# Padded layout for six chunks instead of four, more zero matmuls in the opening, and two weight casts split over two engines

## Chip, cores, metric

The kernel runs on one core of one Trainium2 chip. The metric is device time in microseconds (us) of one execution. Each comparison ran before and changed kernel in turn on one chip. A profile is one execution under the hardware profiler; its "span" is a little shorter than the device time (219.3 against 221.05 us for the profiled run of before).

## The reference, cut to what matters

Block-wise attention with a decay per head is followed by a feed-forward layer with SiLU. There are 4 batches, 8 heads, 768 positions, head size 64; the reference walks blocks of 64 positions.

```python
for b in range(nb):
    intra = einsum('bhic,bhjc->bhij', qb, kb) * Dmask      # scores in the block
    intra = einsum('bhij,bhjd->bhid', intra, vb)
    inter = einsum('bhid,bhde->bhie', qb * lam_pow, kv_state)
    out[:, :, sl] = intra + inter
    kv_state = lam_block * kv_state + einsum('bhsd,bhse->bhde', kb * rev_pow, vb)
...
h = x @ w_in                                               # x is [3072, 512]
out = (h * sigmoid(h)) @ w_out                             # w_in [512, 2048], w_out [2048, 512]
```

## The kernel before

The kernel works on 24 chunks of 128 tokens, six to a batch. The decay sits in the queries and keys beforehand, so a chunk's attention is: transposes of queries and keys ("tq", "tk", "tp"), scores ("sp", then masked into "ss"), state ("kv_ps", moved to "kvbd"), outputs ("op", moved to "xt"). Two heads share the 128 partitions, so keys and values need zeros beside them. There are two layouts:

- Padded: for each head of a pair a full 128-key tile in which the other head is zero ("ktbd"); the values ("vpad") have zero halves. Both score matmuls are 128 columns wide, and one cast puts the values in place.
- Halves: the tiles hold half the keys of both heads. The second matmul of each kind is 64 columns wide, which saves TensorE (in the trace of before these follow each other every 0.029 us, those of 128 columns every 0.056). But the values must be spread by four further VectorE copies a chunk.

The first four chunks use the padded layout (`c < N0`), the others the halves. POOL (GpSimd) clears the buffers in between.

```python
def spread_v(c):                     # halves only: four VectorE copies, 64 x 256 bf16
    if c in vnew:
        vnew.discard(c)
        vb, vh = natb[c][2], vhalf[c % NKV]
        for j in range(2):
            for h in range(2):
                nc.vector.tensor_copy(vh[64*j:64*j+64, :, h, j, :], vb[64*h:64*h+64, :, j, :])

def pe_s(c, j, tag="att"):           # scores
    qt, kt = tr[c]
    a = 0 if c < N0 else 64 * j
    ...
    for p in range(NP):
        lhsT = kt[:, p, j, :] if c < N0 else kt[:, p, j, :, :]
        nc.tensor.matmul(sp[:, p, :], lhsT=lhsT, rhs=qt[:, p, a:], start=True, stop=True)

def clear_halves():                  # POOL, after the first four chunks are issued
    for i in range(NKV):             # four buffers, used in turn: c % NKV
        nc.gpsimd.memset(ktbd[i], 0.0)
        nc.gpsimd.memset(vpad[i], 0.0)
    ...
```

The program order of the opening is written in a string. `z:8` is eight zero matmuls of 512 columns which only keep TensorE busy, `pq`/`pk` prepare queries and keys, `m` masks, `w:0,D` casts the first piece of `w_in` on VectorE (D), `f:part,half` is an opening feed-forward group: `part` picks two of the four chunks, `half` the two weight slices ("pieces" 0 and 1) it needs.

```
z:8 pq:0,1,P pq:0,0,D tq:0,h pk:0,D pk:1,P tk:0,o z:1 kt:0,1,D ...
... m:3,1,D w:0,D d:2 kv:2,A o:2,att x:2,D
d:3 o:3,att f:0,0 x:3,A w:1,D kv:3,A f:0,1 f:1,0 f:1,1 w:2,D w:3,D
```

After the opening come the feed-forward of chunks 0 to 3, then chunks 4 and 5 between its down-projections, then chunks 6 and 7 between the matmuls of the next feed-forward group, and so on:

```python
st_s(5)
vcast(4), vcast(5)
spread_v(4), spread_v(5)
down0(3, 2)
...
st_o(5)
next_prep()                          # POOL: queries and keys of a later chunk
down0(3, 1)
...
stretch((ups(1), 0, 1), ([(vcast, 6), (spread_v, 6)], 0.0, 0.1), (pieces(2), 0.2, 1.15), ...)
```

## Time and profile before

| | |
|---|---|
| device time, median of the first 3 runs (and of 6) | 221.94 us (222.09) |
| profiled span | 219.3 us |
| TensorE busy | 205.9 us |
| TensorE busy in 50-60 us | 6.91 of 10 us |

The head of the profile's page gives each engine's busy time and share of the span:

```profile
span 219.3 us, 4154 instructions
...
PE 205.9 (94%) x1595; PEld 127.4 (58%) x1595; DVE 122.5 (56%) x264; ACT 102.7 (47%) x213; POOL 62.1 (28%) x68
```

PE is TensorE, DVE VectorE, ACT ScalarE. Only some 13 us of TensorE's time are open to this kind of change. The table of stretches says where a good part of them is:

```profile
core 0: us, PE busy (x) PEld busy (x) DVE busy (x) ACT busy (x) POOL busy (x), PEclk, DMA share, GB/s
50.00:60.00 10.00, 6.91 (x74) 4.80 (x71) 8.84 (x20) 4.65 (x10) 4.87 (x5) 1.00 1.29 227
60.00:70.00 10.00, 10.00 (x105) 7.65 (x102) 8.72 (x21) 5.29 (x13) 4.19 (x4) 1.00 1.26 222
```

From 60 us on TensorE is full. The timeline of TensorE (start, duration, instruction; in brackets the idle time before it and what ended it) names the gaps:

```profile
22.07 13.57 PE L417 MATMUL h_ps<-xt,w_in_bf 128*128 128x256 bf16 x72 [0.39 <-DVE w_in_bf L159]
...
50.84 0.55 PE L394 MATMUL op<-ss,vpad 128*128 128x128 bf16 x8 [0.61 <-DVE vpad L274]
...
53.54 0.40 PE L394 MATMUL op<-qt,kvbd 128*128 128x128 bf16 x4 [1.29 <-DVE kvbd L159]
...
59.56 0.51 PE L363 MATMUL sp<-qt,ktbd 128*128 128x128 bf16 x8 [1.16 <-DVE ktbd L159]
```

All four are released by VectorE. The chain of waits shows what VectorE was doing: the copies of chunk 4's and 5's values, one by one (start, duration, step):

```profile
48.77 0.79 DVE vpad L274
...
49.58 0.22 DVE vpad L274
...
49.83 0.95 DVE vpad L274
...
50.81 0.23 DVE vpad L274
```

One copy takes 0.22 us, but two took 0.79 and 0.95. The mixed timeline at chunk 6 shows with what they coincide:

```profile
55.61 1.04 POOL L243 TENSOR_TENSOR qb<-qf,lam_fwd 128x512 bf16<-128x512 f32 x1 [1.35 <-DMA qf<-in_q_dram]
55.90 2.39 DVE L274 COPY vpad<-vb 64x256 bf16<-64x256 bf16 x4
...
56.93 1.04 POOL L237 TENSOR_TENSOR kb<-kf,lam_bwd 128x512 bf16<-128x512 f32 x1 [0.27 <-DMA kf<-in_k_dram]
...
58.32 0.42 DVE L325 COPY qt<-tp 128x512 bf16<-128x512 bf16 x1
```

By the single records of this trace, 57 of the 80 value copies met no POOL instruction and took 0.22 us each. Sixteen began while one ran: fifteen of them ended 0.08 us after it and took 0.84 to 1.09 us, and one took 0.22. Seven had one start beside them and took 0.22. Here four copies of 0.22 us took 2.39 us, and the copy behind them, of chunk 6's transposed queries, waited too.

The second weight piece: the list of transfers, limited to the moment of its issue (14.9 us), gives its time from issue to landing as the last column:

```profile
w_tmp<-in_moe_w_in_dram SPq DMA_DIRECT2D x1, 512.0 KB, 5.3
```

It landed at 20.2 us.

### The profile page before, as it was taken

To read this page: it belongs to the slowest core of one execution; us is meant where nothing else is said; L and a number is where in the kernel's file an instruction comes from. 1 tells how busy PE (TensorE), PEld (TensorE's weight loads), DVE (VectorE), ACT (ScalarE), POOL (GpSimd) and SP (SyncE) were. 2 spreads that over 40 slices of the span, in tenths; PEclk is the share of its full clock that TensorE was granted. 3 is DMA by queue.
4 is the path that set the end of the run, shared out by engine and by line. 5 is a ranking of instruction groups with operands and counts; after the bars stand their busy time and mean duration, and the time that the engine had idled before them with its cause. 6 is when DMAs were issued, how large, how long until landed. Compare 5 with 4: busy or idle time off the path is not lost.

```text
span 219.3 us, 4154 instructions
## 1 busy us (share of the span) xinstructions
PE 205.9 (94%) x1595; PEld 127.4 (58%) x1595; DVE 122.5 (56%) x264; ACT 102.7 (47%) x213; POOL 62.1 (28%) x68
## 2 busy tenths in 40 slices
PE   4878999996799999999999999999999999999993
PEld 1456644553695777775665566556655565566641
DVE  7699555089888768886686564436571341100021
ACT  4685564142673555655554454445445434433300
POOL 7579600716333332323333334203000000000000
PEclk9999999999999999999999999999999999999999
DMA  4999999999999999999999999949510011011112
GB/s 122 242 221 351 381 387 341 263 232 219 234 232 187 215 194 175 220 202 197 190 173 215 240 169 233 201 115 190 107 48 34 14 51 49 0 51 48 48 56 88
DMA packets 97652, 38.03 MB, mean 173 GB/s; under 512 B 86880, under 2 KB 90976, under 8 KB 97632
## 3 DMA queue, kind: packets, MB, share of 16 engines
q1 hardware_dynamic: 97488, 37.76, 81.1%
q8 instruction: 12, 0.20, 0.4%
q14 instruction: 8, 0.07, 0.1%
q10 hardware_dynamic: 144, 0.00, 0.0%
HBM read 27.27 MB, written 6.29 MB: 153 GB/s over the span
## 4 chain that ended last, share of the span: by engine, by line
PE 83%; DVE 10%; ACT 3%; DMA 2%; issue 1%; POOL 1%; DVEq 0%
PE o_ps L443 37%; PE h_ps L417 35%; PE op L394 5%; PE sp L363 4%; DVE ss L370 3%; DVE vpad L274 2%; DMA lam_sb<-in_lam_dram 2%; PE kv_ps L339 2%; ACT g L421 1%; DVE ktbd L159 1%; DVE ob L447 1%; DVE w_in_bf L159 1%; POOL qb L232 1%; DVE vpad L159 1%; ACT L127 1%
## 5 line engine op out<-in xcount | busy, mean ns | idle before, releaser
L421 ACT ACTIVATE g<-h_ps 128x256 bf16<-128x256 f32 (+2 forms) x144 | 65.1, 456 | 79.5 <-PE h_ps L417 78.1
L417 PE MATMUL h_ps<-xt,w_in_bf 128*128 128x256 bf16 (+2 forms) x592 | 99.9, 304 | 1.0 <-DVE w_in_bf L159 0.7
L443 PE MATMUL o_ps<-w_out_bf,g 128*128 128x512 bf16 x384 | 95.8, 379 | 0.2 <-DVE w_out_bf L159 0.2
L417 PEld LDWEIGHTS <-w_in_bf 128*128 128x128 bf16 x592 | 55.4, 98 | 32.6 <-issue 1.3
L443 PEld LDWEIGHTS <-g 128*128 128x128 bf16 x384 | 36.4, 98 | 32.2 <-issue 0.3
L447 DVE COPY ob<-o_ps 128x512 f32<-128x512 f32 x24 | 16.5, 691 | 47.1 <-PE o_ps L443 47.0
L243 POOL TENSOR_TENSOR qb<-qf,lam_fwd 128x512 bf16<-128x512 f32 x18 | 19.0, 1055 | 67.9 <-DMA qf<-in_q_dram 63.3
L370 DVE TENSOR_TENSOR ss<-sp,mask 128x512 bf16<-128x512 f32 (+1 forms) x48 | 25.7, 575 | 17.2 <-PE sp L363 16.5
L274 DVE COPY vpad<-vb 64x256 bf16<-64x256 bf16 x80 | 29.0, 362 | 1.8
L237 POOL TENSOR_TENSOR kb<-kf,lam_bwd 128x512 bf16<-128x512 f32 x23 | 24.3, 1060 | 6.0 <-DMA kf<-in_k_dram 4.1
L159 DVE CAST kvbd<-kv_ps 64x256 bf16<-64x256 f32 x32 | 13.5, 421 | 9.6 <-PE kv_ps L339 9.4
L402 ACT ACTIVATE xt<-op 128x512 bf16<-128x512 f32 x20 | 11.9, 597 | 11.0 <-PE op L394 10.3
L363 PEld LDWEIGHTS <-ktbd 128*128 128x128 bf16 x192 | 11.8, 100 | 6.2 <-DVE ktbd L159 2.9
L363 PE MATMUL sp<-qt,ktbd 128*128 128x128 bf16 (+1 forms) x192 | 13.7, 213 | 1.7 <-DVE ktbd L159 1.6
L394 PE MATMUL op<-ss,vpad 128*128 128x128 bf16 (+1 forms) x192 | 12.5, 208 | 0.6 <-DVE vpad L274 0.6
L157 ACT ACTIVATE vb<-vf 128x512 bf16<-128x512 f32 x20 | 12.5, 624 | 0.7 <-DMA vf<-in_v_dram 0.6
L159 DVE COPY ktbd<-kn 64x512 bf16<-64x512 bf16 x32 | 12.2, 382 | 0.8 <-DMA kn<-kb 0.5
L394 PEld LDWEIGHTS <-vpad 128*128 128x128 bf16 x192 | 10.7, 98 | 1.1 <-DVE vpad L274 0.8
L232 POOL TENSOR_TENSOR qb<-qf,lam_fwd 128x512 bf16<-128x512 f32 x4 | 4.6, 1166 | 16.6 <-DMA qf<-in_q_dram 15.0
L394 PE MATMUL op<-qt,kvbd 128*128 128x128 bf16 x80 | 7.7, 219 | 1.3 <-DVE kvbd L159 1.3
L159 DVE CAST w_in_bf<-w_tmp 128x1024 bf16<-128x1024 f32 x8 | 6.2, 781 | 3.8 <-DMA w_tmp<-in_moe_w_in_dram 3.8
L489 PE MATMUL warm_ps<-kvbd 128*128 128x512 bf16 x11 | 5.3, 632 | 3.2 <-DVE kvbd L108 3.2
(58 smaller groups left out, 85.4 us busy)
## 6 DMA issues: line engine op xcount, KB each, us to landing
kf<-in_k_dram SPq DMA_DIRECT2D x24, 256.0 KB, 4.8
vf<-in_v_dram SPq DMA_DIRECT2D x24, 256.0 KB, 5.1
out_dram<-ob SPq DMA_DIRECT2D x24, 256.0 KB, 3.1
qf<-in_q_dram SPq DMA_DIRECT2D x18, 256.0 KB, 3.7
w_tmp<-in_moe_w_in_dram SPq DMA_DIRECT2D x8, 512.0 KB, 8.6
w_tmp<-in_moe_w_out_dram SPq DMA_DIRECT2D x8, 512.0 KB, 10.1
qf<-in_q_dram SPq DMA_DIRECT2D x3, 512.0 KB, 5.9
qt<-qb SPq DMA_TRANSPOSE x16, 3.7
```

What stands on the lines that cost most here:

```text
L157: nc.scalar.activation(dst, src, AF.Copy)
L159: nc.vector.tensor_copy(dst, src)
L237: VG[e].tensor_tensor(kb, rawk.pop(c).rearrange("s (p j) d -> s p j d", j=2), decay(lam_bwd, c % NB), op=AL.mult)
L243: nc.gpsimd.tensor_tensor(qb, rawq.pop(c).rearrange("s (p j) d -> s p j d", j=2), decay(lam_fwd, c % NB), op=AL.mult)
L274: nc.vector.tensor_copy(vh[64 * j:64 * j + 64, :, h, j, :], vb[64 * h:64 * h + 64, :, j, :])
L363: nc.tensor.matmul(sp[:, p, :], lhsT=lhsT, rhs=qt[:, p, a:], start=True, stop=True)
L370: VG[e].tensor_tensor(ss, sp, m[:, None, :n].to_broadcast([128, 4, n]), op=AL.mult)
L394: nc.tensor.matmul(dst, lhsT=lhsT, rhs=rhs, start=(i == 0), stop=(i >= len(terms) - NP), skip_group_check=True)
L417: nc.tensor.matmul(hp[:, a:z], lhsT=w_in_bf[:, ko, m * 128:(m + 1) * 128], rhs=xt[g][:, ko, a:z], start=(ko == 0 and a == 0), stop=(ko == ...
L421: nc.scalar.activation(gg, hp[:, :n], AF.Silu)
L443: nc.tensor.matmul(o, lhsT=gt[g, ko][:, mt * BLK:(mt + 1) * BLK], rhs=w_out_bf[:, ko, :], start=(ko == 0), stop=(ko == KO_OUT - 1))
L447: nc.vector.tensor_copy(ob, o)
```

## The change

Its intent: take the value copies of chunks 4 and 5 off VectorE; let TensorE reach its full clock, which in before it has from 11.9 us on, sooner and keep it; shorten VectorE's work before the first feed-forward groups. The core of the diff (every other `c < N0` becomes `c < NPAD` likewise):

```diff
+NPAD = 6
-z:8 pq:0,1,P ... pk:1,P tk:0,o z:1 kt:0,1,D ...
+z:15 pq:0,1,P ... pk:1,P z:2 tk:0,o z:2 kt:0,1,D ...        # 26 zero matmuls in all, not 11
-... m:3,1,D w:0,D d:2 kv:2,A o:2,att x:2,D
-d:3 o:3,att f:0,0 x:3,A w:1,D kv:3,A f:0,1 f:1,0 f:1,1 ...
+... m:3,1,D d:2 kv:2,A
+o:2,att x:2,D w:0,DA z:1,o d:3 o:3,att f:0,0 x:3,A w:1,DA kv:3,A f:0,1 f:1,0 f:1,1 ...
+    nc.vector.memset(kvbd[NKV - 1], 0.0)      # the zero tile, now VectorE's first instruction
     nc.gpsimd.memset(ktbd[2], 0.0)
...
     def cast_w(which, i, e="D"):
-        move(e, w_piece(...), wtmp.pop((which, i)))
+        n = dst.shape[1] // len(e)
+        for h, x in enumerate(e):             # "DA": half on VectorE, half on ScalarE
+            move(x, dst[:, n*h:n*h+n, :], t[:, n*h:n*h+n, :])
...
-        a = 0 if c < N0 else 64 * j
+        a = 0 if c < NPAD else 64 * j
...
-    clear_halves()
+    clear_halves(2, 3)
...
     vcast(4), vcast(5)
-    spread_v(4), spread_v(5)
...
     st_o(5)
     next_prep()
+    clear_halves(0, 1)
     down0(3, 1)
...
-    stretch((ups(1), 0, 1), ([(vcast, 6), (spread_v, 6)], 0.0, 0.1), (pieces(2), ...
+    stretch((ups(1), 0, 1), ([(vcast, 6)], 0.0, 0.1), ([(spread_v, 6)], 0.42, 0.42), (pieces(2), ...
```

Buffers 0 and 1 are now in use until chunk 5, so their clearing moves from the opening to a place after chunk 5.

More of the change, by code (lines that the diff above doesn't have):

```diff
@@ L21 @@
 NQ2 = 6
+NPAD = 6
 ORDER = """
-z:8 pq:0,1,P pq:0,0,D tq:0,h pk:0,D pk:1,P tk:0,o z:1 kt:0,1,D qt:0,A kt:0,0,D qt:1,A s:0,1,o tk:1,h m:0,1,D pq:2,0,D
-s:0,0,att z:2 pq:2,1,P kt:1,0,A s:1,0,o tq:2,att kt:1,1,A pk:2,P m:0,0,D qt:2,A s:1,1,h vc:0,A tk:2,att m:1,0,D
-m:1,1,D d:0 qt:3,A pk:3,P kt:2,1,D s:2,1,h kt:2,0,D kv:0,A o:0,att s:2,0,h m:2,1,D tk:3,o m:2,0,D vc:1,A d:1 x:0,A
-kt:3,0,D kv:1,A s:3,0,att o:1,att kt:3,1,D s:3,1,h vc:2,D m:3,0,D vc:3,D x:1,A m:3,1,D w:0,D d:2 kv:2,A o:2,att x:2,D
-d:3 o:3,att f:0,0 x:3,A w:1,D kv:3,A f:0,1 f:1,0 f:1,1 w:2,D w:3,D
+z:15 pq:0,1,P pq:0,0,D tq:0,h pk:0,D pk:1,P z:2 tk:0,o z:2 kt:0,1,D qt:0,A kt:0,0,D qt:1,A s:0,1,o z:1 tk:1,h m:0,1,D
+pq:2,0,D s:0,0,att z:2 pq:2,1,P kt:1,0,A s:1,0,o tq:2,att kt:1,1,A pk:2,P m:0,0,D qt:2,A s:1,1,h vc:0,A tk:2,att
+m:1,0,D m:1,1,D d:0 qt:3,A pk:3,P kt:2,1,D s:2,1,h kt:2,0,D kv:0,A o:0,att s:2,0,h m:2,1,D z:1,o tk:3,o m:2,0,D vc:1,A
+z:2,o d:1 x:0,A kt:3,0,D kv:1,A s:3,0,att o:1,att kt:3,1,D s:3,1,h vc:2,D m:3,0,D vc:3,D x:1,A m:3,1,D d:2 kv:2,A
+o:2,att x:2,D w:0,DA z:1,o d:3 o:3,att f:0,0 x:3,A w:1,DA kv:3,A f:0,1 f:1,0 f:1,1 w:2,D w:3,D
 """
@@ L106 @@
         nc.vector.memset(vpad[i], 0.0)
-        if i == 1:
-            nc.vector.memset(kvbd[NKV - 1], 0.0)
         nc.vector.memset(ktbd[i], 0.0)
@@ L161, in cast_w @@
     def cast_w(which, i, e="D"):
-        move(e, w_piece(which, i, None, w_in_bf if which == "in" else w_out_bf), wtmp.pop((which, i)))
+        dst, t = w_piece(which, i, None, w_in_bf if which == "in" else w_out_bf), wtmp.pop((which, i))
+        n = dst.shape[1] // len(e)
+        for h, x in enumerate(e):
+            move(x, dst[:, n * h:n * h + n, :], t[:, n * h:n * h + n, :])
     mask2 = const.tile([128, BLK], F32)
@@ L170, with clear_halves @@
     khalf = [t.rearrange("d p j s -> d p (j s)").rearrange("d p (h j s) -> d p h j s", h=2, j=2) for t in ktbd]
-    def clear_halves():
-        for i in range(NKV):
+    def clear_halves(*bufs):
+        for i in bufs:
             nc.gpsimd.memset(ktbd[i], 0.0)
             nc.gpsimd.memset(vpad[i], 0.0)
-        for j in range(2):
-            nc.gpsimd.tensor_copy(mask2[64 * j:64 * j + 64, :], mask[0:64, :])
     NBUF = {"att": 3, "h": 2, "o": 2, "kv": 1}
@@ L190 @@
     xt = {}
-    N0 = GROUPS[0] // BLK
     def load_q(c):
@@ L238, in prep_k @@
                                 op=AL.mult)
-        natb[c] = (None, kb, vpad[c % NKV] if c < N0 else nat.tile([128, NP, 2, D], BF16, name="vb", tag="vb", bufs=2))
+        natb[c] = (None, kb, vpad[c % NKV] if c < NPAD else nat.tile([128, NP, 2, D], BF16, name="vb", tag="vb", bufs=2))
     def prep(c):
@@ L248, in vcast @@
     def vcast(c, e="A"):
-        if c in vraw and c >= N0:
+        if c in vraw and c >= NPAD:
             vb = natb[c][2]
@@ L284, in move_k @@
         rows = slice(64 * j, 64 * j + 64)
-        if c < N0:
+        if c < NPAD:
             move(e, ktbd[c % NKV][rows, :, j, :], t[rows, :, :])
@@ L304, in copy_qt @@
              tp[:, :, :, 64 * i:64 * i + 64].rearrange("d r p s -> d p s r"))
-        tr[c] = (qt, ktbd[c % NKV] if c < N0 else khalf[c % NKV])
+        tr[c] = (qt, ktbd[c % NKV] if c < NPAD else khalf[c % NKV])
     def pe_tk(c, tag):
@@ L338, in pe_d @@
         for p in range(NP):
-            nc.tensor.matmul(kv[:, p, :], lhsT=kb[:, p, :, :], rhs=vb[:, p, 0:4:3, :] if c < N0 else vb[:, p, :, :],
+            nc.tensor.matmul(kv[:, p, :], lhsT=kb[:, p, :, :], rhs=vb[:, p, 0:4:3, :] if c < NPAD else vb[:, p, :, :],
                              start=(blk == 0 and p == 0), stop=True, skip_group_check=True)
@@ L358, in pe_s @@
         qt, kt = tr[c]
-        a = 0 if c < N0 else 64 * j
+        a = 0 if c < NPAD else 64 * j
         sp = psum.tile([128, NP, BLK - a], F32, name="sp", tag=tag, bufs=NBUF[tag], padded_shape=[128, NP, BLK])
         for p in range(NP):
-            lhsT = kt[:, p, j, :] if c < N0 else kt[:, p, j, :, :]
+            lhsT = kt[:, p, j, :] if c < NPAD else kt[:, p, j, :, :]
             nc.tensor.matmul(sp[:, p, :], lhsT=lhsT, rhs=qt[:, p, a:], start=True, stop=True)
@@ L374, in st_s @@
         spread_k(c)
-        st[c] = [masked(pe_s(c, j), m=mask2) for j in range(2)]
+        st[c] = [masked(pe_s(c, j), m=mask if c < NPAD else mask2) for j in range(2)]
     def pe_o(c, tag="att"):
@@ L387, in pe_o @@
         for j in range(2):
-            if c < N0:
+            if c < NPAD:
                 terms += [(vb[:, p, 2 * j:2 * j + 2, :], res[j][:, p, :], op[:, p, :]) for p in range(NP)]
@@ L514, in next_prep @@
                 load_c(loads.pop(0))
-    clear_halves()
+    clear_halves(2, 3)
+    for j in range(2):
+        nc.gpsimd.tensor_copy(mask2[64 * j:64 * j + 64, :], mask[0:64, :])
     for i in range(4, 8):
@@ L594, in stretch @@
             fn(*args)
-    stretch((ups(1), 0, 1), ([(vcast, 6), (spread_v, 6)], 0.0, 0.1), (pieces(2), 0.2, 1.15),
+    stretch((ups(1), 0, 1), ([(vcast, 6)], 0.0, 0.1), ([(spread_v, 6)], 0.42, 0.42), (pieces(2), 0.2, 1.15),
             (downs(1, range(1)), 1, 1.5))
```

## The prediction

> **What bounds it now.** The page gives a span of 219.3 us, TensorE busy for 205.9 (94%); from 60 us on it is full (table of stretches). A gain can only come from its idle 13 us. The timeline shows where: (a) Opening: the first feed-forward group starts at 20.64 and the next waits until 22.07 for the second weight piece; the chain of waits from 10.3 to 22.0 lies almost wholly on VectorE. (b) Chunks 4 and 5: TensorE is busy 6.9 of 50-60, with gaps of 0.6 (vpad), 1.3 (kvbd) and 1.2 us (ktbd), all released by VectorE. The chain there runs through VectorE's vpad copies: 3.3 us for the eight of chunks 4 and 5, 2.4 us for chunk 6's four; one takes 0.22 us alone, up to 1.07 while POOL works.
>
> **Mid section.** The padded layout takes the eight copies off the chain (-3.3 us of VectorE). It adds two wider mask multiplies (a pair takes 1.29 instead of 1.02 us) and about 0.4 us of TensorE (16 matmuls of 128 instead of 64 columns). Following the order with these durations, chunk 5's outputs no longer wait for kvbd, and the last down-projection ends about 53.1 instead of 55.15, the start unchanged: -2.0. Moving chunk 6's copies behind its scores lets its transposes be evacuated at once: scores start 3.4 instead of 4.6 us into the stage, -1.1. Against it: POOL's four memsets of buffers 0 and 1 (0.95 us each) now fall near 54-58 us, beside chunk 6's copies, and push chunk 8's preparation back. [...] I expect chunk 6's copies to take 1-2.5 us and cost 0-2 us before chunk 7's scores: +0.8.
>
> **Opening.** Early zero matmuls run 0.43 us each, later ones 0.22; four transposes take 0.61, and 0.39 us after 11.5 us. [...] two latencies of 0.2 us off the chain before 10. POOL clears half as much, so the cast of chunk 2's values should fall from 0.94 to about 0.53. Splitting two weight casts saves VectorE about 0.4 us each; the second piece lands about 20.2. I expect the second feed-forward group about 21.1. But chunk 4's queries land only at 39.66, so its transposes can't start before about 41.75 (42.55 now): the opening is worth at most 0.8, I take 0.7.
>
> **Sum.** 0.7 + 2.0 + 1.1 - 0.8 - 0.1 (matmuls not yet counted) = 2.9. With some discount: **219.2 us**, range 218.0 to 220.8; chances: faster by over 2% 0.04, within 2% 0.95, slower 0.01.
>
> **What would show it.** No vpad copies before 54 us, TensorE busy about 9 of 50-60; the kvbd gap gone; chunk 6's score gap under 0.5; zeros at 0.22 us by 7 us; second feed-forward group about 21.1; chunk 4's transposes about 41.8, waiting for POOL; then a uniform shift of 2.5-3 us, no new gaps.
>
> **What would make it wrong.** POOL's memsets block VectorE's copies for all of 3.8 us, so that chunk 6 or 7 gives the gain back; chunk 8's late preparation stalls the load queue and starves later chunks; the zeros stay cold and hold back the first transposes; the opening gain is lost waiting for chunk 4's queries. If the copies suffer nothing, 218 is possible.

The sum came to 0.7 + 2.0 + 1.1 - 0.8 - 0.1 = 2.9 us. The full clock was to come early in the opening, with zero matmuls at 0.22 us by 7 us: that was the author's estimate, and before had not shown it. Before's eight zero matmuls from 3.15 us had not brought that clock, and all its eleven, which end before 11.9 us, run at 0.43 us where one follows another; those of the changed kernel run at 0.22 from 5.5 us on. The "two latencies of 0.2 us" are the difference between four of before's transposes at first and after 11.5 us, 0.61 and 0.39 us.

## The result

| | before | changed |
|---|---|---|
| device time, median of 6 runs | 222.09 us (221.34 to 222.58) | 220.27 us (219.65 to 220.59) |
| profiled span | 219.3 us | 218.9 us |

The ratio is 0.9914 (95% interval 0.9891 to 0.9938), within 2%. A ratio here is the mean time of one kernel's fast runs over that of the other's of the same rounds, so it is not quite the ratio of the medians. The same program run again as a control (e5 below) had 0.9939 (0.9907 to 0.9970). So the gain is 0.6 to 0.9%, 1.4 to 1.9 us, against 2.7 predicted.

The two traced runs differ by only 0.4 us of span. The traced run of the changed kernel was the slowest of its six, and the traced one of before, at 221.05 us, was faster than its median. I use traces for where, not for how much in total.

The profile after, page head:

```profile
span 218.9 us, 4179 instructions
...
PE 208.1 (95%) x1610; PEld 128.0 (58%) x1610; DVE 114.1 (52%) x256; ACT 103.7 (47%) x215; POOL 60.2 (28%) x68
```

The same two stretches, same columns:

```profile
50.00:60.00 10.00, 9.36 (x98) 7.23 (x97) 6.04 (x13) 5.47 (x13) 8.05 (x9) 1.00 1.04 220
60.00:70.00 10.00, 8.91 (x87) 6.26 (x85) 8.29 (x23) 4.36 (x11) 3.40 (x4) 1.00 1.02 232
```

The middle filled, from 6.91 to 9.36 us, but the stretch behind it, which had been full, lost 1.1 us. TensorE's timeline:

```profile
22.24 13.57 PE L419 MATMUL h_ps<-xt,w_in_bf 128*128 128x256 bf16 x72 [1.02 <-DVE w_in_bf L160]
...
57.50 0.51 PE L365 MATMUL sp<-qt,ktbd 128*128 128x128 bf16 x8 [0.41 <-DVE ktbd L160]
...
61.69 0.29 PE L396 MATMUL op<-ss,vpad 128*128 128x64 bf16 x4 [0.16 <-DVE vpad L276]
...
63.78 0.51 PE L365 MATMUL sp<-qt,ktbd 128*128 128x128 bf16 x8 [0.93 <-DVE ktbd L160]
```

The gaps at chunks 4 and 5 are gone and that before chunk 6's scores fell from 1.16 to 0.41 us. There are two new things: a gap of 1.02 us (0.39 in before) ahead of the second feed-forward group, and gaps before chunk 7. VectorE and then POOL around chunks 6 and 7:

```profile
58.93 2.70 DVE L276 COPY vpad<-vb 64x256 bf16<-64x256 bf16 x4
...
62.88 0.85 DVE L160 COPY ktbd<-tp 64x512 bf16<-64x512 bf16 x2
```

```profile
54.70 0.95 POOL L179 MEMSET ktbd<- 128x1024 bf16 x1
55.59 0.95 POOL L180 MEMSET vpad<- 128x1024 bf16 x1
56.48 0.95 POOL L179 MEMSET ktbd<- 128x1024 bf16 x1
57.37 0.95 POOL L180 MEMSET vpad<- 128x1024 bf16 x1
58.29 1.04 POOL L245 TENSOR_TENSOR qb<-qf,lam_fwd 128x512 bf16<-128x512 f32 x1
59.29 1.04 POOL L239 TENSOR_TENSOR kb<-kf,lam_bwd 128x512 bf16<-128x512 f32 x1
60.50 1.05 POOL L245 TENSOR_TENSOR qb<-qf,lam_fwd 128x512 bf16<-128x512 f32 x1 [0.17 <-DMA qf<-in_q_dram]
```

POOL's memsets run before chunk 6's copies start. What the copies meet is POOL's preparation of chunk 8, which the memsets pushed back to 58.29 us (in before it was done at 58.0), and the first multiply for chunk 9, which came when it did in before (60.50 against 60.58 us).

The second weight piece, issued at the same time as before:

```profile
w_tmp<-in_moe_w_in_dram SPq DMA_DIRECT2D x1, 512.0 KB, 6.7
```

It now landed at 21.6 instead of 20.2 us.

The starts of some matmuls in the two traced runs, in us, give the account:

| | before | changed | difference | the step alone | predicted for it |
|---|---|---|---|---|---|
| scores of chunk 4 | 45.11 | 45.18 | +0.07 | +0.07 | -0.7 |
| next feed-forward stage | 54.97 | 53.31 | -1.66 | -1.73 | -2.0 |
| scores of chunk 6 | 59.56 | 57.50 | -2.06 | -0.40 | -1.1 |
| scores of chunk 7 | 64.42 | 63.78 | -0.64 | +1.42 | +0.8 |
| scores of chunk 8 | 72.04 | 71.42 | -0.62 | +0.02 | 0 |

### The profile page after: what moved, and what is told of

It reads as the page before. It is cut to its first block, busy times and chain, and to the rows that moved or that the text cites. A ratio compares the mean times of both kernels' runs of the same rounds, so it can differ in the third digit from the quotient of the medians.

```text
span 218.9 us, 4179 instructions
## 1 busy us (share of the span) xinstructions
PE 208.1 (95%) x1610; PEld 128.0 (58%) x1610; DVE 114.1 (52%) x256; ACT 103.7 (47%) x215; POOL 60.2 (28%) x68
## 4 chain that ended last, share of the span: by engine, by line
PE 68%; DVE 3%; ACT 1%; issue 1%
PE o_ps L445 32%; PE h_ps L419 28%; PE op L396 4%; PE sp L365 3%; PE kv_ps L341 1%; DVE vpad L276 1%; ACT xt L404 1%; DVE ktbd L160 1%; DVE kvbd L160 0%; DVE ob L449 0%; ACT g L423 0%; DVE ss L372 0%; DVE qt L327 0%
## 5 line engine op out<-in xcount | busy, mean ns | idle before, releaser
L372 DVE TENSOR_TENSOR ss<-sp,mask 128x512 bf16<-128x512 f32 (+1 forms) x48 | 26.2, 586 | 18.9 <-PE sp L365 17.7
L276 DVE COPY vpad<-vb 64x256 bf16<-64x256 bf16 x72 | 24.0, 334 | 1.6
L404 ACT ACTIVATE xt<-op 128x512 bf16<-128x512 f32 x20 | 11.9, 597 | 9.6 <-PE op L396 9.0
L365 PEld LDWEIGHTS <-ktbd 128*128 128x128 bf16 x192 | 11.3, 98 | 6.4 <-DVE ktbd L160 3.3
L160 DVE COPY ktbd<-kn 64x512 bf16<-64x512 bf16 x32 | 10.4, 324 | 3.2 <-DMA kn<-kb 2.9
L158 ACT ACTIVATE vb<-vf 128x512 bf16<-128x512 f32 x18 | 11.2, 623 | 0.0
L491 PE MATMUL warm_ps<-kvbd 128*128 128x512 bf16 x26 | 9.0, 474 | 1.3 <-DVE kvbd L104 1.3
L160 DVE CAST w_in_bf<-w_tmp 128x1024 bf16<-128x1024 f32 (+1 forms) x8 | 5.2, 644 | 5.9 <-DMA w_tmp<-in_moe_w_in_dram 5.9
L341 PEld LDWEIGHTS <-kb 128*128 128x128 bf16 x80 | 6.1, 98 | 3.3 <-issue 0.9
```

The lines of the kernel that those rows point to most:

```text
L160: nc.vector.tensor_copy(dst, src)
L276: nc.vector.tensor_copy(vh[64 * j:64 * j + 64, :, h, j, :], vb[64 * h:64 * h + 64, :, j, :])
L372: VG[e].tensor_tensor(ss, sp, m[:, None, :n].to_broadcast([128, 4, n]), op=AL.mult)
L404: nc.scalar.activation(xt[g][:, :, off * BLK:(off + 1) * BLK], op, AF.Copy)
```

## Experiments

All kernels computed the right result. Each was timed in five rounds; ratios are to the kernel before in the same rounds, whose median was 221.25 to 221.53 us in these sessions. The theory: the layout gives about 2 us and loses some of it at chunk 7 to POOL; the opening is worth nothing because of the second weight piece's landing. The first rival: the opening is worth its 0.7 us, and the middle less.

### e1: the layout alone

Edit: the changed kernel with the order string, `cast_w` and first memset of before.

> The layout part alone (first six chunks padded, clearing of buffers 0 and 1 and the copies of chunk 6 moved), with the opening of before. Theory A (the opening part is bounded by the landing of the second weight piece and gains nothing; all of the gain is in the middle): ratio to before equal to that of the whole change, 0.991 within 0.002, about 220.2 us. Rival B (the opening gains 0.7 us in a typical run, the middle less than was predicted): ratio about 0.994 to 0.995.

Measured: ratio 0.9965 (0.9929 to 1.0001), median 220.37 us. Four of the six runs took 219.75 to 220.45, two 221.69 and 221.91 us. The ratio is above both expectations, and the times can't separate the two theories. The traced run had the second weight piece at 20.14 us, and had chunk 6's scores at 57.05 but chunk 7's at 63.81: 6.76 us between them, against 4.86 in before.

What the layout is worth in the middle is plain from all traces taken together. From chunk 4's scores to the next feed-forward stage it took 8.13 or 8.14 us in each of the twelve traces with the padded layout, whatever their opening, and 9.86 (before) and 9.75 us (e2) in the two without it.

### e2: the opening alone

Edit: before with the new order string, split casts and first memset.

> The opening part alone (more zero matmuls, the zero tile written first, two weight casts split over two engines, the new order), with the layout of before. Theory A: ratio 0.999 to 1.001; the second feed-forward group starts no earlier than about 0.6 us after its weight piece lands, and chunk 4's transposes stay at about 42.5 us. Rival B: ratio about 0.997, that is 0.7 us less, with the second group at about 21.1 us.

Measured: ratio 0.9986 (0.9963 to 1.0009), median 221.23 us. The piece landed at 21.44 us, and chunk 4's scores started at 45.44 (45.11 in before). By this ratio the opening is worth about 0.3 us; both zero and the rival's 0.997 are inside the interval. The trace is against the rival. The first piece was late too (19.45 instead of 18.81), and the first feed-forward group started at 21.23 instead of 20.64. Nor did the new opening bring chunk 4's scores forward elsewhere: in the other fast traces with its order (changed, e3, e7, e8) they start at 45.01 to 45.27 us, with the old one at 45.11 (before) and 44.73 (e1).

### e3: chunk 6's copies back at their old place

```diff
-    ([(vcast, 6)], 0.0, 0.1), ([(spread_v, 6)], 0.42, 0.42)
+    ([(vcast, 6), (spread_v, 6)], 0.0, 0.1)
```

> The changed kernel, with the copies of chunk 6's values put back to where they were, ahead of chunk 6's transposes on VectorE. If moving them behind the scores was worth the predicted 1.1 us minus the loss at chunk 7 (0.8): 0.3 us slower than the changed kernel, ratio to before 0.992 to 0.994. If POOL's memsets block the copies there for up to 2.7 us and the scores of chunk 6 wait: 1 to 2 us slower than the changed kernel, ratio 0.996 to 1.0. If the move only shifted the wait from chunk 6 to chunk 7: no difference, ratio 0.991.

Measured: ratio 1.0175 (1.0150 to 1.0199), median 225.40 us, beyond all three expectations. VectorE's line, then TensorE's, of the timeline:

```profile
54.21 6.15 DVE L276 COPY vpad<-vb 64x256 bf16<-64x256 bf16 x4
```

```profile
61.64 0.82 PE L365 MATMUL sp<-qt,ktbd 128*128 128x128 bf16 x8 [4.81 <-DVE ktbd L160]
```

Four copies of 0.22 us took 6.15 us behind POOL's four memsets and two multiplies; by the records of the single copies the first, started at 54.21, ended at 58.11, after all four memsets: one copy was held for 3.90 us. TensorE waited 4.81 us, and during the wait, at 59.94 us, its clock fell. The seventh value after the time range of a stretch is the granted clock:

```profile
60.00:64.00 4.00, 2.36 (x17) 1.87 (x18) 2.54 (x7) 0.38 (x1) 2.13 (x3) 0.50 1.08 288
64.00:67.00 3.00, 3.00 (x23) 2.49 (x22) 0.84 (x2) 1.15 (x3) 0.00 (x0) 0.54 0.69 151
```

It stood at half for 6.83 us by the clock records. So moving these copies behind the scores is not a fine point of the change: with the memsets at their new place it is necessary. In this trace the memsets hold up VectorE's value copies (3.90 us for one) as POOL's multiplies do in before (up to 1.09 us).

### e4: second and third feed-forward groups exchanged

```diff
-f:0,0 x:3,A w:1,DA kv:3,A f:0,1 f:1,0 f:1,1
+f:0,0 x:3,A w:1,DA kv:3,A f:1,0 f:0,1 f:1,1
```

> The changed kernel, with the second and third of the four opening feed-forward groups exchanged, so that the second group uses the first weight piece again (on the other two chunks) and the second piece is needed 0.87 us later. Theory A (landing of the second piece bounds the opening): TensorE's gap of about 1.0 us before the second group shrinks to about 0.3, chunk 4's transposes come up to 0.45 us earlier (their queries then land too late for more), ratio to before 0.988 to 0.990. Rival B (VectorE's order bounds it): no gain, 0.991.

Measured: ratio 0.9923 (0.9900 to 0.9947), median 220.03 us. The weight piece landed late again (21.40), but the gap before the second group is gone. Chunk 4's transposes then wait for their queries:

```profile
42.02 0.62 PE L299 MATMUL tq<-ident,qb 128*128 128x128 bf16 x8 [0.25 <-POOL qb L234]
```

The opening was bounded by that landing, and right behind it stands the landing of chunk 4's queries, as the prediction had said. By time alone e4 is not told apart from the changed kernel; the ratio of 0.988 to 0.990 that theory A promised did not come.

### e5: the changed kernel again

Edit: an empty line.

> The changed kernel again, unchanged but for an empty line, as a control on this chip and in these rounds: ratio to before 0.991 within 0.002, with the second weight piece landing at about 21.5 us and the gap before chunk 7's scores at about 0.9 us.

Measured: ratio 0.9939 (0.9907 to 0.9970), somewhat above what was expected, median 220.06 us, but one run took 222.95, and it was the profiled one, slow (over 1.5% above the fastest). Its stretches show the clock at half:

```profile
64.00:66.00 2.00, 1.34 (x12) 1.16 (x13) 1.87 (x7) 0.68 (x2) 0.00 (x0) 0.69 0.73 159
66.00:68.00 2.00, 1.78 (x11) 1.35 (x11) 1.04 (x3) 0.77 (x2) 0.66 (x1) 0.50 1.24 241
```

Chunk 6's copies took 3.61 us there, TensorE had gaps of 0.29, 0.61 and 0.93 us before chunk 7, and the clock then fell to half for 3.41 us. As that run is slow, it is not used for any difference. The gaps alone do not explain the fall: in e9, a fast run, TensorE had gaps of 0.38, 0.70 and 0.93 us at the same place, and the clock stayed full. What made the two long runs of e1 stays open, since those were not traced.

### e6: few zero matmuls

```diff
-z:15 ... z:2 tk:0,o z:2 ... z:1,o tk:3 ... z:2,o d:1 ... z:1,o d:3
+z:8 ... tk:0,o ... tk:3 ... d:1 ... d:3
```

> The changed kernel with the zero matmuls of before (11 instead of 26) and everything else of the opening kept. Theory C: [...] then this kernel has [...] the piece at about 20.2, the second feed-forward group at 20.8-21.1 and 0.3 to 0.6 us less than the whole change. Rival D: the later landing is made by splitting the casts or by something else of the opening: the piece still lands at 21.4 or later and the time is that of the whole change or longer, as the clock comes later.

Measured: ratio 0.9961 (0.9934 to 0.9987), median 220.46 us. The piece landed earlier, at 20.98 us, and the gap before the second group went, but there was no gain. The full clock came at 12.8 us instead of 5.5, four transposes took 0.61 instead of 0.40 us, and the first state matmuls started at 14.49 instead of 13.88. So the kernel came to its feed-forward at 20.61 instead of 20.18 us and had less use of the earlier piece. Theory C took the 15 added zero matmuls to be what makes the piece late; how they were to do it, no trace shows. It is borne out by half: without them the piece landed earlier, but at 20.98 and not at about 20.2. Fifteen of its parts were there by 20.17; the last one was late before the first of the packets that are looked at below (21.05 us). The gain is not borne out.

### e9: only the first fifteen zero matmuls

```diff
-z:15 ... z:2 tk:0,o z:2 ... z:1 tk:1,h ... (every later z)
+z:15 ... tk:0,o ... tk:1,h ...
```

> The changed kernel with only the first 15 zero matmuls; the 11 placed between the later steps of the opening are taken out. Theory C [...]: [...] the second weight piece lands at 20.2 to 21.0 us; the clock still comes at 4 to 7 us; the second feed-forward group starts at 20.8 to 21.3, 0.2 to 0.6 us less than the whole change. Rival E: the later zeros hold the clock up; without them it falls back to half before the feed-forward or the chain of the opening lengthens, and the kernel is as slow as the whole change or slower.

Measured: ratio 0.9989 (0.9961 to 1.0016), median 220.94 us, so the rival is right: the clock, granted at 4.4 us, fell back.

```profile
11.00:14.00 3.00, 2.15 (x20) 1.93 (x21) 2.65 (x4) 1.22 (x3) 1.98 (x2) 0.54 1.39 218
14.00:18.00 4.00, 3.40 (x30) 2.82 (x29) 3.06 (x7) 3.17 (x7) 1.99 (x2) 0.50 1.25 247
```

In the ten other traces with fifteen zeros at the start, which keep the later ones, it did not fall in the opening: in these traces the small zero groups between the steps hold the clock up (0.54 and 0.50 in the two stretches above without them, 1.00 in both in the changed kernel with them). In this trace the piece landed at 20.57 us, but the feed-forward began only at 21.56.

### What delays the second weight piece

The landing records give 16 parts to a weight piece. A cast waits for the last of them: in the changed kernel the second piece's last part landed at 21.62 us, and both halves of its cast started at 21.64. The packet records show 12 packets of 16384 bytes (0.20 MB) in a run, in the queue that the page lists as "q8 instruction". What they are for, and which engine they serve, is in no record. I set them beside TensorE's progress, as they seem to follow it: in all 14 traces 461 to 465 of its recorded matmuls and weight loads had started before the second packet, and 235 to 289 before the first. This table is drawn from those records:

```
                          first such packet    second weight piece
                          after the start, us  landed, us
before                    20.22                20.20
e1 layout alone           20.25                20.14
e6 few zeros              21.05                20.98
e9 first zeros only       22.02                20.57
changed                   19.12                21.62
e2 opening alone          18.06                21.44
e3 copies 6 early         19.54                21.72
e4 groups exchanged       18.02                21.40
e5 changed again          18.16                21.52
e7 clear early            17.75                21.11
e8 eight padded chunks    18.26                21.47
e10                       18.15                21.50
e11                       19.07                21.64
e12 casts unsplit         17.74                21.24
```

In before the packet comes behind the second piece: there the third piece has 15 parts landed by 21.68 and one at 22.60. In the changed kernel it comes ahead: of the second piece 14 parts landed by 20.11, the last two at 20.87 and 21.62. In e4, e5, e10 and e12 just one part was late: fifteen were there by 20.09 to 20.16, the last at 21.24 to 21.52. In the ten traces with all the extra zero matmuls the packet came 0.7 to 2.5 us sooner than in before. The first such packet took 0.93 to 1.11 us, and where it came before 20 us the piece landed 0.9 to 1.5 us later than in before. In all 14 traces the piece landed at 21.1 us or later where the packet came before 20 us, and before 21 us where it came after. The two groups are only 0.13 us apart there, because of e6's late part. That the number of zero matmuls moves the landing is shown (e6, e9), and that the split of the casts does not make it late (e12); that the packet is what does it was the author's reading of these coincidences and is not shown, as no run moved the packet alone. One of the two late parts of the changed kernel, like e6's, goes with no recorded packet, and what made it stays open.

### e12: the casts not split

```diff
-w:0,DA ... w:1,DA
+w:0,D ... w:1,D
```

> The changed kernel with the first two weight casts whole on VectorE instead of split over VectorE and ScalarE. Theory: the second group waits for the landing of the second piece (21.4-21.7 us), so the split only shortens the cast after it (0.54-0.63 instead of about 0.8 us): the second group starts 0.2 to 0.3 us later, 22.4 to 22.6, and the kernel is 0.1 to 0.3 us slower than the whole change, not to be told apart from it by time (ratio to before 0.990 to 0.996). Rival: VectorE's order bounds the opening as predicted, the split is worth 0.8 us: ratio 0.996 to 0.998, second group at 22.8 or later.

Measured: ratio 0.9960 (0.9925 to 0.9995), median 220.87 us, between the two expectations. The second group:

```profile
22.74 13.57 PE L419 MATMUL h_ps<-xt,w_in_bf 128*128 128x256 bf16 x72 [1.28 <-DVE w_in_bf L160]
```

It is 0.5 us later than with the split. The piece had landed at 21.24, 1.50 us before, against 0.62 us in the changed kernel: the whole cast took 1.42 us beside POOL's memsets, the half casts 0.54 and 0.63. That is as much as the rival gave the split (0.8). But in e7, with the split, 1.07 us passed, so it is not always so much. By time it is not told apart from the control.

### e7: clearing early, with two more buffer pairs

```diff
+    for i in range(2):                         # padded buffers of chunks 4 and 5
+        vpad.append(const.tile(...)); ktbd.append(const.tile(...))
+    def pbuf(c):
+        return c if c < NPAD else c % NKV
...
     clear_halves(2, 3)
     ...                                        # mask copy
+    for i in range(2):
+        nc.gpsimd.memset(ktbd[NKV + i], 0.0); nc.gpsimd.memset(vpad[NKV + i], 0.0)
+    clear_halves(0, 1)
...
     next_prep()
-    clear_halves(0, 1)
```

The activation pool has 31 instead of 33 tiles to make room.

> The changed kernel with two further pairs of padded buffers for chunks 4 and 5, cleared by POOL in its idle time after 22 us, and buffers 0 and 1 cleared there too, so that no memset is left at 54-58 us (31 instead of 33 activation tiles make the room). Theory: the memsets push POOL's preparation of chunks 8 and 9 against chunk 6's copies, which take 2.7 us and hold up chunk 7's scores; without them the copies take 1 to 1.5 us, the gap of 0.9 us before chunk 7's scores goes, 0.7 to 1.2 us less than the whole change. Rival: POOL's multiplies for chunks 8 and 9 hold the copies up as much by themselves: copies still over 2 us, less than 0.3 us gained.

Measured: ratio 0.9903 (0.9875 to 0.9930), median 219.21 us, its six runs within 218.92 to 219.63. POOL, VectorE, and the stretch that had lost 1.1 us:

```profile
57.41 1.04 POOL L246 TENSOR_TENSOR kb<-kf,lam_bwd 128x512 bf16<-128x512 f32 x1
60.08 1.04 POOL L252 TENSOR_TENSOR qb<-qf,lam_fwd 128x512 bf16<-128x512 f32 x1 [1.63 <-DMA qf<-in_q_dram]
```

```profile
58.82 0.94 DVE L283 COPY vpad<-vb 64x256 bf16<-64x256 bf16 x4
...
61.00 0.85 DVE L167 COPY ktbd<-tp 64x512 bf16<-64x512 bf16 x2
```

```profile
60.00:70.00 10.00, 9.95 (x96) 7.23 (x95) 6.90 (x20) 4.88 (x12) 3.56 (x4) 1.00 1.18 212
```

TensorE's scores of chunks 6 and 7:

```profile
57.45 0.51 PE L372 MATMUL sp<-qt,ktbd 128*128 128x128 bf16 x8 [0.41 <-DVE ktbd L167]
...
62.30 0.50 PE L372 MATMUL sp<-qt,ktbd 128*128 128x128 bf16 x8
```

POOL is free when the copies come (58.45 to 60.08). They take 0.94 us, and chunk 7's scores follow chunk 6's by 4.85 us, as in before (4.86). With chunk 6's scores at the same place as in the changed kernel (57.45 against 57.50), this isolates the loss: it was POOL's displaced work. In time, e7's median is 0.85 us under that of the control of the same rounds; the two intervals overlap, but e7's slowest run (219.63) is below all of the control's but one (219.45).

### e8: eight padded chunks

```diff
-NPAD = 6
+NPAD = 8
...
-    clear_halves(2, 3)
...
         fns[kind](c)
+        if kind == "o" and c == NPAD - 1:
+            clear_halves(2, 3)
```

(The transposes of chunks 6 and 7 take the padded tiles likewise.)

> The changed kernel with chunks 6 and 7 in the padded layout too: no vpad copies before chunk 8 (eight fewer, 1.9 us alone, 3.6 us as they ran), two mask multiplies wider by 0.27 us, about 0.4 us more of TensorE; buffers 2 and 3 cleared after chunk 7. If VectorE's copies are what gives the gain back at chunk 7: both gaps before chunk 7's outputs and scores (0.2 and 0.9 us) go and the kernel is 0.7 to 1 us faster than the whole change. If the gain is lost elsewhere by the time of chunk 8 (loads, preparation): the same as the whole change or slower by the 0.4 us of matmuls.

Measured: ratio 0.9905 (0.9880 to 0.9930), median 219.28 us. There are no value copies before chunk 8, and no gap before chunk 7; its scores start at 62.19 us. POOL's memsets and multiplies run back to back there as in the changed kernel, and harm nothing. So it takes both, the copies and the displaced POOL work, to lose the time. Its median is 0.78 us under the control's, again with intervals that overlap.

### e10 and e11: two versions put together

e10 is e7, e11 is e8, each with the exchanged groups of e4 and with chunk 4's queries loaded before the sixth piece of `w_out` instead of behind it.

> A proposed version: the early clearing with the two further buffer pairs, the exchanged second and third feed-forward groups, and chunk 4's queries loaded one weight piece earlier. If the gains add: 0.5 us from the opening on top of the 0.9 of the early clearing, 218.4 to 218.9 us, ratio 0.986 to 0.988. If the wait for chunk 4's keys or for VectorE takes the opening's share: no better than the early clearing alone, 0.990.

Measured: ratio 0.9889 (0.9871 to 0.9906), median 218.73 us (218.46 to 219.01). The opening runs through:

```profile
20.11 15.05 PE L426 MATMUL h_ps<-xt,w_in_bf 128*128 128x256 bf16 x80
```

> The other proposed version: eight padded chunks, the exchanged groups, and chunk 4's queries loaded one weight piece earlier. If the gains add: 218.4 to 219.0 us, ratio 0.986 to 0.989; if not, 0.990.

Measured: ratio 0.9898 (0.9876 to 0.9920), median 219.01 us. Both beat before. e10's median is 1.3 us under the control's, and its interval ends just below where the control's begins (0.9906 against 0.9907), though it overlaps that of the first measurement of the change (0.9891 to 0.9938); the rounds were others. Over e7 and e8 the gains of e10 and e11 are inside the intervals, so that the opening's part adds is not shown.

## Why the prediction was right or wrong

The class (within 2%) and the range (218.0 to 220.8) held: 220.27 us. The point, 219.2, was too low by 1.1. All four terms came out less well than predicted, so no errors cancelled; the range held because it was wide, and because the timed gain is larger than the sum of the traced pair, which is luck as far as the argument goes. By terms of its sum:

- **Mid section, -2.0.** Right in mechanism, nearly in size: -1.73 in the trace. The kvbd gap is gone, TensorE is busy 9.36 of 50-60 us (predicted about 9), and no vpad copies run before 54 us.
- **Chunk 6's scores, -1.1.** Wrong in size: -0.40. The gap fell to 0.41 us as predicted ("under 0.5"), but the transposes started 2.30 us into the stage (53.31 to 55.61), where I had counted 1.75 (16 matmuls at 0.108; the sum, scores 3.4 us into the stage, became 4.19); in before it was 1.95. TensorE waited there for ScalarE (0.20 us are listed), which had the cast of chunk 6's values in between. The copy behind them started 0.65 us after the transposes, where I had counted 0.5. These 0.7 us are the term's error.
- **Copies of chunk 6, +0.8.** Right in mechanism, too small: they took 2.70 us ("1 to 2.5") and the step to chunk 7's scores grew by 1.42. In the other fast traces with this part of the program unchanged (e1, e4, e6, e9, e12) the step was 5.65 to 7.37 us, that is 0.8 to 2.5 more than before's 4.86. e7 removes the cause and the step is 4.85. What I named, the memsets beside the copies, was not quite it: the memsets were over by then, and the multiplies that they had delayed met the copies. In the changed trace, too, every copy that began while a POOL instruction ran ended 0.08 us after it: 11 of its 72, which took 0.48 to 1.11 us (the 57 that met none took 0.22 to 0.23). e3's 6.15 us for four copies of 0.22 agrees on the waiting, but there the first copy ended only after four memsets that had all started later than it.
- **Opening, -0.7.** The step that failed. "The second piece lands about 20.2" was read from before, and I took it as fixed. With the added zero matmuls it landed at 21.6, the second group started at 22.24 instead of 21.1, and chunk 4's scores were no earlier (+0.07). The parts inside were right: zeros at full clock before 7 us (from 5.5), transposes at 0.40 us, the cast of chunk 2's values at 0.43 instead of 0.94 (predicted 0.53). They shortened a chain that then waited for a load. Why the load was late is not shown, as said above. e2 puts the opening at 0.1% with zero inside the interval; it loses its worth if the later zeros go (e9).
- **"Then a uniform shift, no new gaps."** No: two new gaps, as above.

The terms of the traced pair sum to 0.6 us at chunk 8, less than the 1.4 to 1.9 of the timed runs. The larger part of what is missing, 1.0 us, lies with before: its traced run, at 221.05 us, was faster than all of its six timed ones (221.34 to 222.58). The loss at chunk 7 varies between traces; whether untraced runs lose less there is not shown.

The runs' own records of the clock belong here too. Of the 46 timed runs of before in the experiments' sessions, 26 had a mean granted clock of 0.992 or less, and the nine at 0.985 averaged 222.56 us, against 221.16 for the twenty at 0.996 or more; the traced run had 1.000 (the figure leaves out the start: full clock came there only at 11.9 us). Of the twelve timed runs of the changed kernel and of e2, none was below 0.996. So a part of the timed gain may be clock that the new opening keeps, which the traced pair can't show. Its size stays open: in e6 the three runs at 0.984 were no slower than the others.

## What to carry to other kernels

When work is taken off one engine, look at what the same change moves onto an engine that the remaining work was seen to wait for: copies of 0.22 us turned into a wait of 0.9 us because four memsets on an idle engine delayed that engine's other work into them. A landing time read from a trace holds for that program only: here a change of TensorE's zero matmuls made a load late that everything waits for (21.62 instead of 20.20 us), by a way that is not shown. Idle engines are free only where nothing later queues behind the work one gives them; clearing in POOL's idle time from 22 us on, with two more buffers, was worth what clearing at 54 us had cost.

## What the traces show of the clock, and what stays open

- When it falls. In e3 the clock fell 3.1 us into a gap of 4.81 us, and stood at half for 6.83 us. But it also fell with no such gap: in e9 at 11.26 us, after a stretch (8 to 11 us) in which TensorE was busy for 1.66 of 3 us and had no gap above 0.52 us; in e5's slow run at 64.8 us after gaps of 0.29, 0.61 and 0.93 us. Nor does the share of busy time sort the cases: e9 kept the full clock from 62 to 70 us, although TensorE was busy for only 2.20 of the first 4 us. What decides stays open. The clock stayed at half for 6.83 us in e9 and 3.41 us in e5.
- When it comes. In before, eight zero matmuls lasting 3.60 us did not bring the full clock (it came at 11.9 us); in e1, with the same eight, it came at 6.7. With fifteen it came at 4.0 to 6.7 us in the eleven traces that have them: a block of nearly twice as many zero matmuls was enough in each of these traces.
